# Sliding-window attention and a gated feed-forward block on one core: attention matmuls recut into 64x64 tiles, chunks 2 to 7 transposed on TensorE, output blocks moved later

## The chip, the cores and the metric

The kernel runs on one core of a Trainium2 chip. The core has TensorE (PE, matmuls; its weight loads are listed as PEld), VectorE (DVE), ScalarE (ACT), GpSimd (POOL) and SyncE (SP), and 16 DMA engines that all queues share. PE writes to eight PSUM banks of 128 partitions x 512 f32, which DVE and ACT read; everything else works on SBUF, 128 partitions wide. The metric is the device time of one execution in microseconds (us).

## The reference

```python
# q, k, v: (8, 8, 576, 64): batch, heads, positions, head size
scores = q @ k^T / 8, masked to 0 <= i - j < 64
attn   = softmax(scores)
x      = (attn @ v) laid out as 4608 tokens x 512
g      = x @ w_gate                      # 512 x 1536
out    = (g * sigmoid(g) * (x @ w_val)) @ w_out     # 1536 x 512, float32
```

All inputs and the output are float32 in memory; the kernel computes with bfloat16 operands and float32 sums.

## The kernel before

**Chunks and blocks.** The 4608 tokens are 36 chunks of 128 (n = 0 to 35) for the attention and 9 blocks of 512 (c = 0 to 8) for the feed-forward. A chunk holds all 8 heads.

**Attention of a chunk.** `S(n)` (L340) makes the scores transposed, keys on the partitions. For each half chunk of 64 queries (w) the window is the 128 keys from 64 before it; 16 matmuls hold 64 rows (head size) x 128 keys as weights and stream 64 queries. Even and odd heads (p) stand in the two halves of the rows and write two banks. ACT takes the exponential (L373), DVE multiplies by the 0/1 mask (L375); in the first four chunks a mask of -30000 is added by a matmul instead (L354). `AV(n)` (L377) has 16 matmuls of 128x128 weights (the probabilities) against 65 columns of v (64 and a column of ones): for each head one on `vb` (the values shifted by 64 tokens, L390) and one on `va` (L391). DVE takes the reciprocal of the sum (L397) and multiplies (L400) into `xb`. The probabilities are kept 192 wide with a zero middle so that both matmuls have all 128 columns. `X(n)` (L403) turns `xb` into a quarter of `xT`: by four PE transposes and a copy in the first six chunks, by a DMA transpose on SP's queue (L412) from chunk 6 on. `T(n)` (L324) turns k and q by DMA transposes on SP's queue (L332), from chunk 4 on; `shift_v` (L290) makes `vb` by two SP DMAs a chunk. The first two pairs of chunks are loaded as float32, cast, and transposed on PE (`first_loads`, `first_cast`, `first_T`).

**Feed-forward.** `F(c, f)` (L504) makes one of 12 row blocks of the hidden layer for 512 tokens: 4 + 4 matmuls of 512 columns (L479), tanh on ACT (L490), two DVE operations (L498, L501) into `hT`. `O(c, u)` (L528) makes 128 rows of the output: 12 matmuls (L538), a copy on ACT (L543), an ACT-queue DMA. `hT` is a ring of two (`NH`), so all of block c-1's outputs are made while block c is computed.

**Order.** The order on each engine is written out by hand in `opening` (L573) and `build` (L636); `_Graph` (L31) derives the semaphore waits from which buffer is read and written, and an instruction that waits holds everything behind it on its engine or queue. POOL's queue carries the float32-to-bfloat16 loads (k, q and v at L288, the two weights at L313, `Wo` at L318) in program order; a load waits for the last reader of its ring slot. SP's queue carries the transposes and the shifted values in order. In the main loop (blocks 2 to 8) each quarter u has F, AV(n), F, S(n+1), O(c-1, u), F on PE. PSUM banks: four for F, one for O (`"o"`), three for attention (`"a"`).

Of the kernel before, what the change touches and what calls it, by code (L numbers as in the profile page):

```python
# [9 lines left out]
T = B * S  # L10
# [20 lines left out]
class _Graph:  # L31
# [10 lines left out]
    def op(self, eng, fn, reads=(), writes=(), dma=False):  # L42
# [4 lines left out]
        for k in writes:  # L47
            for r in self.readers.get(k, ()):
                deps.setdefault(r.i, (r, "war"))
            for w in self.writers.get(k, ()):  # L50
                deps.setdefault(w.i, (w, "waw"))
        o = _Op(len(self.ops), eng, fn, list(deps.values()), dma)
# [8 lines left out]
    def emit(self):  # L61
# [7 lines left out]
        for o in self.ops:  # L69
# [16 lines left out]
            for d, kind in deps:  # L86
                if d.eng == e and not d.dma and (e == "pe" or kind != "raw") and not o.dma and e != "pool":
                    continue
                need(d)
# [60 lines left out]
class _Kernel:  # L150
# [5 lines left out]
    NH = 2  # L156
    NS = 4
    NO = 4

# [6 lines left out]
    def alloc(self):  # L166
# [9 lines left out]
        self.mask = sb("mask", 4 * 64)  # L176
        self.nmask = sb("nmask", 4 * 64)
# [3 lines left out]
        hd = lambda t: t[:, :].rearrange("p (h d) -> p h d", h=H)  # L181
        self.qn = ring("qn", self.NQ, DM)
        self.kn = ring("kn", self.NQ, DM)
        self.va = [hd(t) for t in ring("va", self.NV, H * 80)]
        self.vb = [hd(t) for t in ring("vb", self.NV, H * 80)]
        self.kT = sb("kT", 4 * (T + 64))[:, :].rearrange("p (c t) -> p c t", c=4)
        self.qT = sb("qT", 4 * self.NZ * 128)[:, :].rearrange("p (c t) -> p c t", c=4)
        self.wz = sb("wz", 512)
        self.pt = [t[:, :].rearrange("p (h x) -> p h x", h=H) for t in ring("pt", self.NP, H * 192)]
# [10 lines left out]
        self.fk = [f4(hT[1][:, 0:2048]), f4(hT[1][:, 2048:4096])]  # L200
        self.fq = [f4(hT[1][:, 4096:6144]), f4(xT[2][:, :])]
        h1 = lambda a: [("hT", 1, f) for f in range(4 * a, 4 * a + 4)]
        self.fkk = [h1(0), h1(1)]
        self.fqk = [h1(2), [("xT", 2, u) for u in range(4)]]
        c4 = lambda t: t[:, :].bitcast(BF).rearrange("p (j h d) -> p j h d", j=4, h=4)
        self.ck, self.cq = [c4(self.ost[0]), c4(self.ost[2])], [c4(self.ost[1]), c4(self.ost[3])]
        self.ckk, self.cqk = [[("ost", 0)], [("ost", 2)]], [[("ost", 1)], [("ost", 3)]]
        self.wup = sb("wup", 1, F32)
        self.ps = [nc.alloc_psum_tensor("ps%d" % i, [128, 512], F32) for i in range(8)]
        self.rot = {"f": ([0, 1, 2, 3], 0), "o": ([4], 0), "a": ([5, 6, 7], 0)}  # L210
# [28 lines left out]
    def init(self):  # L239
        g = self.g  # L240
        self.zero(self.wup[:, :], ["wup"])
        g.op("act", lambda e: e.activation(self.wup[:, :], self.wup[:, :], ACTF.Exp), writes=["wup"])
        self.zero(self.ident[:, :], ["ident"])
        self.zero(self.wz[:, :], ["wz"])
        self.zero(self.nmask[:, :], ["nmask"])
        self.init_va(0, 4)
        self.zero(self.kT[:, :, 0:64], [("kT", -1, 0), ("kT", -1, 1)])
        self.zero(self.vb[0][0:64, :, 0:66], [("vb", 0, 0)])
        for i in range(self.NP):
            self.zero(self.pt[i][:, :, 64:128], [("pt", i, 0), ("pt", i, 1)])  # L250
        self.zero(self.mask[:, :], ["mask"], 1.0)
# [5 lines left out]
    def init_ident(self, m, key):  # L257
        self.g.op("pool", lambda e: e.affine_select(
            out=m[:, :], in_=m[:, :], compare_op=ALU.not_equal, fill=1.0, base=0,
            pattern=[[-1, 128]], channel_multiplier=1), writes=[key])  # L260

    def init_mask(self, m, key, fill):
        mm = m[:, :].rearrange("p (a q) -> p a q", a=4)
        self.g.op("pool", lambda e: e.affine_select(
            out=mm, in_=mm, compare_op=ALU.is_gt, fill=fill, base=0,
            pattern=[[0, 4], [-1, 64]], channel_multiplier=1), writes=[key])
        self.g.op("pool", lambda e: e.affine_select(
            out=mm, in_=mm, compare_op=ALU.is_ge, fill=fill, base=64,
            pattern=[[0, 4], [1, 64]], channel_multiplier=-1), writes=[key])
        self.g.op("pool", lambda e: e.memset(m[0:64, 128:192], fill), writes=[key])  # L270
# [19 lines left out]
    def shift_v(self, n, eng="sp"):  # L290
        if n >= NCH:
            return
# [484 lines left out]
```

## Time and profile before

| What | us |
|---|---|
| Three runs | 366.23, 367.96, 367.74; median 367.74 |
| Span of the profiled execution (its own time) | 366.3 |
| PE busy | 335.8 (92%), 2617 matmuls |
| DVE / ACT / POOL busy | 223.2 (61%) / 131.5 (36%) / 108.7 (30%) |
| Matmuls of F (L479) | 116.3 + 115.6 |
| Matmuls of O (L538) | 96.1 |
| Matmuls of S (L360), of AV (L390, L391) | 15.3; 23.1 + 23.2 |
| Mean granted TensorE clock | 0.971 |

The profiled execution took as long as the fastest of the three runs; its span runs from the first to the last instruction. Busy time of PE counts overlapping matmuls once, and a matmul's record includes its way through the array, so a record of 0.19 us does not keep the next matmul waiting for 0.19 us: the distance between starts does. "issue" in a chain is time in which the engine waited for nothing that the profile shows. Times in the timeline are from the start of the span.

### The profile page before, as it was taken

Reading aid. Unit: us, or ns where it says so; the run is one execution under the profiler, and the core shown is the slowest. Engines: PE = TensorE matmul, PEld = TensorE weight load, DVE = VectorE, ACT = ScalarE, POOL = GpSimd, SP = SyncE. Lnnn points to the kernel's source line nnn. Section 1 sums busy time; section 2 is a strip of 40 time slices with the busy share of each in tenths; the row PEclk is TensorE's granted clock in tenths of the full one; section 3 lists DMA queues with packets and bytes.
Section 4 is the critical chain, followed back from the end, with each engine's and each line's share of the span. In section 5 each row is a group of like instructions: output and inputs, shape, how many; then the busy total and the mean of one; then the engine's idle time right before and its main releaser. Section 6 shows DMA issues by size and latency. Waiting matters only on the chain.

```text
span 366.3 us, 6689 instructions
## 1 busy us (share of the span) xinstructions
PE 335.8 (92%) x2617; PEld 170.8 (47%) x2617; DVE 223.2 (61%) x482; ACT 131.5 (36%) x234; POOL 108.7 (30%) x139
## 2 busy tenths in 40 slices
PE   7677976399859999899999999999999999999996
PEld 3354445365424444444444444444444444444444
DVE  5667887346446666666666666666666666545530
ACT  2343433124332343344433433334344433233221
POOL 8999614252055432222222433220000000000000
PEclk9789998889988999999999999999999999999999
DMA  9999999999999999999999999996433332101003
GB/s 161 227 182 153 180 183 147 156 173 188 163 169 164 162 152 137 155 134 130 149 143 147 149 132 145 140 144 103 91 90 91 95 77 44 44 35 54 29 29 117
DMA packets 176864, 47.30 MB, mean 129 GB/s; under 512 B 159360, under 2 KB 172352, under 8 KB 176832
## 3 DMA queue, kind: packets, MB, share of 16 engines
q0 software_dynamic: 113152, 17.83, 69.8%
q1 hardware_dynamic: 57952, 19.20, 31.6%
q10 hardware_dynamic: 5728, 9.83, 7.8%
q8 instruction: 21, 0.34, 0.4%
q14 instruction: 11, 0.09, 0.1%
HBM read 37.75 MB, written 9.44 MB: 129 GB/s over the span
## 4 chain that ended last, share of the span: by engine, by line
PE 83%; DVE 6%; DMA 6%; issue 3%; ACT 2%; SPq 1%; ACTq 0%; DVEq 0%
PE ps L479 48%; PE ps L538 25%; DMA qT<-qn 4%; PE ps L360 3%; PE ps L391 2%; PE ps L390 2%; DMA hT<-in_q_dram 2%; DVE xb L400 2%; DVE uu L498 1%; ACT sig L490 1%; PE ps L560 1%; DVE vb L234 1%; DVE kT L234 1%; PE ps L354 1%; DVE hT L501 1%
## 5 line engine op out<-in xcount | busy, mean ns | idle before, releaser
L498 DVE SCALAR_TENSOR_TENSOR uu<-sig,ps 128x512 bf16<-128x512 bf16 (+1 forms) x116 | 75.1, 647 | 96.7 <-ACT sig L490 96.2
L479 PE MATMUL ps<-xT,Wg 128*128 128x512 bf16 (+1 forms) x472 | 116.3, 370 | 9.6 <-issue 5.5
L479 PE MATMUL ps<-xT,Wv 128*128 128x512 bf16 (+1 forms) x472 | 115.6, 369 | 0.0
L490 ACT ACTIVATE sig<-ps 128x512 bf16<-128x512 f32 (+1 forms) x116 | 65.9, 568 | 115.2 <-PE ps L479 115.2
L538 PE MATMUL ps<-Wo,hT 128*128 128x512 bf16 x420 | 96.1, 380 | 0.0
L501 DVE SCALAR_TENSOR_TENSOR hT<-uu,ps 128x512 bf16<-128x512 bf16 (+1 forms) x116 | 75.4, 650 | 4.5 <-PE ps L479 0.5
L479 PEld LDWEIGHTS ps<-xT,Wv 128*128 128x128 bf16 x472 | 47.3, 100 | 49.2 <-issue 1.9
L479 PEld LDWEIGHTS ps<-xT,Wg 128*128 128x128 bf16 x472 | 44.0, 100 | 52.8 <-issue 7.7
L538 PEld LDWEIGHTS ps<-Wo,hT 128*128 128x128 bf16 x420 | 39.2, 98 | 44.9
L288 POOL DMA_DIRECT2D qn<-in_q_dram x36 | 30.3, 843 | 84.6 <-DMA qT<-qn 82.9
L373 ACT ACTIVATE pt<-ps 128x512 bf16<-128x512 f32 x72 | 39.0, 595 | 33.4 <-PE ps L360 32.9
L543 ACT ACTIVATE ost<-ps 128x512 f32<-128x512 f32 x35 | 20.9, 597 | 67.0 <-PE ps L538 67.0
L288 POOL DMA_DIRECT2D kn<-in_k_dram x36 | 30.4, 846 | 43.7 <-DMA kT<-kn 40.8
L288 POOL DMA_DIRECT2D va<-in_v_dram x40 | 34.3, 861 | 7.4 <-DMA Wo<-in_moe_w_out_dram 4.7
L400 DVE TENSOR_TENSOR xb<-ps,rc 128x256 bf16<-128x256 f32 x72 | 30.6, 425 | 2.5
L375 DVE TENSOR_TENSOR pt<-pt,mask 128x512 bf16<-128x512 bf16 x64 | 24.8, 420 | 11.2 <-ACT pt L373 10.7
L360 PE MATMUL ps<-qT,kT 64*128 64x64 bf16 x576 | 15.3, 195 | 9.2 <-issue 3.9
L390 PE MATMUL ps<-vb,pt 128*128 128x65 bf16 x288 | 23.1, 195 | 0.3 <-ACT pt L373 0.3
L391 PE MATMUL ps<-va,pt 128*128 128x65 bf16 x288 | 23.2, 195 | 0.0
L390 PEld LDWEIGHTS ps<-vb,pt 128*128 128x128 bf16 x288 | 20.7, 99 | 4.1 <-ACT pt L373 0.5
L360 PEld LDWEIGHTS ps<-qT,kT 64*128 64x128 bf16 x576 | 11.0, 97 | 23.7 <-DVE rc L397 9.8
L391 PEld LDWEIGHTS ps<-va,pt 128*128 128x128 bf16 x288 | 19.5, 99 | 3.4
(48 smaller groups left out, 76.9 us busy)
## 6 DMA issues: line engine op xcount, KB each, us to landing
out_dram<-ost ACTq DMA_DIRECT2D x35, 256.0 KB, 2.8
vb<-va SPq DMA_DIRECT2D x63, 80.0 KB, 3.3
va<-in_v_dram POOLq DMA_DIRECT2D x32, 128.0 KB, 6.4
kn<-in_k_dram POOLq DMA_DIRECT2D x28, 128.0 KB, 5.7
qn<-in_q_dram POOLq DMA_DIRECT2D x28, 128.0 KB, 4.9
Wo<-in_moe_w_out_dram POOLq DMA_DIRECT2D x2, 768.0 KB, 26.3
Wg<-in_moe_w_gate_dram POOLq DMA_DIRECT2D x5, 256.0 KB, 9.7
Wv<-in_moe_w_val_dram POOLq DMA_DIRECT2D x5, 256.0 KB, 11.3
```

The lines of the kernel that those rows point to most:

```text
L288: self.g.op("pool", lambda e, d=d, a=a: e.dma_start(d, a), writes=ks, dma=True)
L360: r = e.matmul(sv[p][:, w, c], self.kT[ps, c, k0:k0 + 128], self.qT[ps, c, self.qs(n, 64 * w, 64 * w + 64)], start=not bias, stop=not bias ...
L373: g.op("act", lambda e, po=po, p=p: e.activation(po, sv[p], ACTF.Exp, scale=SCALE), reads=[bx[p][1]], writes=[pk])
L375: g.op("dve", lambda e, po=po: e.tensor_tensor(po, po, m, ALU.mult), reads=[pk, "mask"], writes=[pk])
L390: e.matmul(av[:, j, :], pt[:, h, 0:128], vb[:, h, 0:65], start=True, stop=False)
L391: r = e.matmul(av[:, j, :], pt[:, h, 64:192], va[:, h, 0:65], start=False, stop=True)
L400: g.op("dve", lambda e, xo=xo, av=av, rb=rb: e.tensor_tensor(xo, av[:, :, 0:64], rb, ALU.mult), reads=[bk, ("rc", ir)], writes=[("xb", ix, ...
L479: r = e.matmul(bank[:, lo:hi], W[:, kk, f * 128:f * 128 + 128], xT[:, kk, lo:hi], start=(kk == 0), stop=(kk == NK - 1))
L490: self.g.op("act", lambda e: e.activation(sig[:, lo:hi], G[:, lo:hi], ACTF.Tanh, scale=0.5), reads=[gk], writes=[("sig", i)])
L498: g.op("dve", lambda e: e.scalar_tensor_tensor(uu[:, lo:hi], sig[:, lo:hi], 1.0, G[:, lo:hi], ALU.add, ALU.mult), reads=[("sig", i), gk], ...
L501: g.op("dve", lambda e: e.scalar_tensor_tensor(hT[:, f, lo:hi], uu[:, lo:hi], 0.5, V[:, lo:hi], ALU.mult, ALU.mult), reads=[("uu", i), vk] ...
L538: r = e.matmul(OB[:, :], hT[:, f, 128 * u:128 * u + 128], self.Wo[:, f, :], start=(f == 0), stop=(f == NF - 1))
```

## The change

- **64x64 tiles.** S has, for each pair of heads, one matmul of the chunk's first 64 keys against all 128 queries into the lower half of the partitions, and two of 64 keys (the last 64 of the chunk before, the last 64 of this one) against 64 queries each into the upper half: 24 matmuls of 64x64 weights. Keys no longer need a window that starts 64 early, so `kT` becomes a ring of eight chunks. AV has 32 matmuls of 64x64 weights in two phases of 16. Within a phase each half of the rows writes one bank; in the second phase the banks are exchanged, and its first matmul waits on PE's own semaphore until the first phase is done. `vb` and `shift_v` go: the values of the chunk before are read from `va`.
- **B(n)** puts S(n+1) between the two phases of AV(n), from chunk 8 on.
- **Chunks 2 to 7.** k and q are loaded two tokens to a partition (`load2`) and transposed on PE (`T2`: 16 transposes and two copies for each of k and q of two chunks). The float32 path is kept for chunks 0 and 1 alone. X of chunks 4 to 7 is by PE, its copy on ACT.
- **F** can take a half of the tokens for two row blocks at once, which share one bank, one tanh and one DVE pair; chunks 0 to 3 and block 1 are ordered by such halves.
- **Three hT.** O(0,0) closes block 1; after that the outputs run up to seven quarters behind, and six outputs and the divided last one stand at the end. The bank of O joins those of attention.
- **Loads** are put in another order: all gate and value weights before k and q of chunks 4 and 5; `Wo` behind the loads of chunks 8 to 11.

```diff
@@ op, emit @@
-    def op(self, eng, fn, reads=(), writes=(), dma=False):
+    def op(self, eng, fn, reads=(), writes=(), dma=False, after=None):
...
+        if after is not None:
+            deps[after.i] = (after, "sync")
...
-                if d.eng == e and not d.dma and (e == "pe" or kind != "raw") and not o.dma and e != "pool":
+                if d.eng == e and not d.dma and kind != "sync" and (e == "pe" or kind != "raw") and not o.dma and e != "pool":
...
-    NH = 2
+    NH = 3
...
-        self.vb = [hd(t) for t in ring("vb", self.NV, H * 80)]
-        self.kT = sb("kT", 4 * (T + 64))[:, :].rearrange("p (c t) -> p c t", c=4)
+        self.qs2 = [pair(t) for t in ring("qs", 2, 2 * DM)]
+        self.ks2 = [pair(t) for t in ring("ks", 2, 2 * DM)]
+        self.kT = sb("kT", 4 * self.NZ * 128)[:, :].rearrange("p (c t) -> p c t", c=4)
-        self.rot = {"f": ([0, 1, 2, 3], 0), "o": ([4], 0), "a": ([5, 6, 7], 0)}
+        self.rot = {"f": ([0, 1, 2, 3], 0), "a": ([4, 5, 6, 7], 0)}
...
-    def shift_v(self, n, eng="sp"):
...
+    def load2(self, st, x):
+        src, dst = (self.k, self.ks2[st % 2]) if x == "k" else (self.q, self.qs2[st % 2])
+        parts = list(self.segs(256 * st, 256))
+        for j, (r, b, s, L) in enumerate(parts):
+            d = dst[r // 2:(r + L) // 2].rearrange("p h j d -> p h (j d)")
+            a = src[b, :, s:s + L, :].rearrange("h (p j) d -> p h (j d)", j=2)
+            ks = [("s2", x, st % 2, j)] if len(parts) > 1 else [("s2", x, st % 2, 0), ("s2", x, st % 2, 1)]
+            self.g.op("pool", lambda e, d=d, a=a: e.dma_start(d, a), writes=ks, dma=True)
...
+    def T2(self, st, x, engs):
+        g = self.g
+        src = (self.ks2 if x == "k" else self.qs2)[st % 2]
+        dst = self.kT if x == "k" else self.qT
+        z0 = (2 * st) % self.NZ
+        for cc in range(2):
+            bank, bk = self.bank("a")
+            tb = bank[:, 0:256].bitcast(BF).rearrange("p (c j t) -> p c j t", c=2, j=2)
+
+            def pe(e, cc=cc, tb=tb):
+                for c in range(2):
+                    for j in range(2):
+                        for p in range(2):
+                            r = e.transpose(tb[64 * p:64 * p + 64, c, j, :], src[:, 4 * cc + 2 * c + p, j, :], self.ident[:, :])
+                return r
+
+            g.op("pe", pe, reads=["ident", ("s2", x, st % 2, 0), ("s2", x, st % 2, 1)], writes=[bk])
+            d = dst[:, 2 * cc:2 * cc + 2, 128 * z0:128 * z0 + 256].rearrange("p c (t j) -> p c t j", j=2)
+            a = tb.rearrange("p c j t -> p c t j")
+            self.copy(engs[cc], d, a, [bk], [(x + "T", z, cc) for z in (z0, z0 + 1)])
...
-            for w in range(2):
-                k0 = 128 * n + 64 * w
-                for c in range(4):
+                    e.matmul(sv[p], self.ident[:, :], nm, start=True, stop=False, skip_group_check=True)
+            kw = dict(start=not bias, stop=True, skip_group_check=True)
+            for c in range(4):
+                for p in range(2):
+                    ps = slice(64 * p, 64 * p + 64)
+                    e.matmul(sv[p][0:64, c, :], self.kT[ps, c, self.zs(n, 0, 64)], self.qT[ps, c, self.zs(n)], **kw)
+                for ks, a in ((lk, 0), (self.zs(n, 64, 128), 64)):
                     for p in range(2):
                         ps = slice(64 * p, 64 * p + 64)
-                        r = e.matmul(sv[p][:, w, c], self.kT[ps, c, k0:k0 + 128],
-                                     self.qT[ps, c, self.qs(n, 64 * w, 64 * w + 64)],
-                                     start=not bias, stop=not bias or (w == 1 and c == 3))
+                        r = e.matmul(sv[p][64:128, c, a:a + 64], self.kT[ps, c, ks], self.qT[ps, c, self.zs(n, a, a + 64)], **kw)
             return r
...
-    def AV(self, n):
...
-                    e.matmul(av[:, j, :], pt[:, h, 0:128], vb[:, h, 0:65], start=True, stop=False)
-                    r = e.matmul(av[:, j, :], pt[:, h, 64:192], va[:, h, 0:65], start=False, stop=True)
...
+    def AVmm(self, st, phase):
+        n, bx, av, done = st
+        iv, jv, ip = n % self.NV, (n - 1) % self.NV, n % self.NP
+        va, vb, pt = self.va[iv], self.va[jv], self.pt[ip]
+
+        def pe(e):
+            for j in range(4):
+                for r in range(2):
+                    p = r if phase == 0 else 1 - r
+                    h = 2 * j + p
+                    for c in range(2):
+                        if n == 0 and r == 1 and c == 0:
+                            continue
+                        first = j == 0 and (phase == 0 or (n == 0 and c == 0 and r == 0))
+                        rows = slice(64 * r, 64 * r + 64)
+                        vv = vb if (r == 1 and c == 0) else va
+                        x = e.matmul(av[p][64 * c:64 * c + 64, j, :], pt[rows, h, 64 * c:64 * c + 64], vv[rows, h, 0:65],
+                                     start=first, stop=phase == 1, skip_group_check=True)
+            return x
+
+        rd = [("pt", ip, 0), ("pt", ip, 1)]
+        for i in {iv, jv} if n else {iv}:
+            rd += [("va", i), ("va", i, 0), ("va", i, 1)]
+        done.append(self.g.op("pe", pe, reads=rd, writes=[b[1] for b in bx], after=done[0] if phase else None))
...
+    def B(self, n):
+        st = self.AVa(n)
+        self.AVmm(st, 0)
+        if n + 1 < NCH:
+            self.S(n + 1)
+        self.AVmm(st, 1)
+        self.AVn(st)
...
-    def Fmm(self, bank, bk, W, wk, c, f, lo, hi):
...
-    def Fa(self, c, f):
...
-    def Fb(self, c, f, b):
...
+    def F(self, c, fs, half=None):
+        g = self.g
+        lo, hi = (0, 512) if half is None else (256 * half, 256 * half + 256)
...
-        OB, ok = self.bank("o")
+        OB, ok = self.bank("a")
...
+    def loads(self):
         W = lambda a, b: (self.load_w("g", a, b), self.load_w("v", a, b))
+        kq = lambda st: (self.load2(st, "k"), self.load2(st, "q"))
+        self.first_loads()
         self.init()
         self.load(0, "v")
         self.load(1, "v")
+        self.init_ident()
         W(0, 2)
+        self.init_mask()
+        kq(1)
+        W(2, 4)
         self.load(2, "v")
         self.load(3, "v")
         W(4, 6)
         W(6, 8)
+        W(8, 10)
+        W(10, 12)
+        kq(2)
+        self.load(4, "v")
         self.load(5, "v")
...
+    def more_loads(self):
+        self.load2(3, "k")
+        self.load2(3, "q")
+        self.load(6, "v")
+        self.load(7, "v")
+        for n in range(8, 12):
+            self.load(n)
         self.load_wo(0, 6)
         self.load_wo(6, 12)
-        self.load(8)
-        self.load(9)
-
+        self.load(12)
...
+        F(0, (0, 1), 0)
+        T2(1, "k", ("act", "dve"))
+        T2(1, "q", ("act", "dve"))
+        F(0, (2, 3), 0)
+        S(2, True)
+        S(3, True)
+        AV(2)
+        X(2, "act")
+        AV(3)
+        X(3, "act")
         self.init_va(4, self.NV)
+        self.more_loads()
+        F(0, (4, 5), 0)
+        F(0, (0, 1), 1)
+        F(0, (6, 7), 0)
+        F(0, (2, 3), 1)
+        F(0, (4, 5), 1)
+        F(0, (6, 7), 1)
+        T2(2, "k", ("act", "act"))
+        T2(2, "q", ("act", "act"))
+        F(0, (8,))
+        S(4)
+        S(5)
+        F(0, (9,))
+        AV(4)
+        AV(5)
         self.load(13)
+        F(0, (10,))
+        X(4, "act")
+        X(5, "act")
+        F(0, (11,))
+        F(1, (0, 1), 0)
+        T2(3, "k", ("act", "act"))
+        T2(3, "q", ("act", "act"))
+        F(1, (2, 3), 0)
+        S(6)
+        S(7)
+        for n in (8, 9):
+            self.T(n, "k")
+            self.T(n, "q")
+        F(1, (4, 5), 0)
+        AV(6)
+        AV(7)
+        F(1, (6, 7), 0)
+        X(6, "act")
+        X(7, "act")
+        F(1, (8, 9), 0)
+        self.T(10, "k")
+        self.T(10, "q")
+        F(1, (10, 11), 0)
+        F(1, (0, 1), 1)
+        S(8)
+        F(1, (2, 3), 1)
+        self.B(8)
+        self.X(8)
+        self.T(11, "k")
+        self.T(11, "q")
+        F(1, (4, 5), 1)
+        self.B(9)
+        self.X(9)
+        self.T(12, "k")
+        self.T(12, "q")
+        self.load(14)
+        F(1, (6, 7), 1)
+        self.B(10)
+        self.X(10)
+        self.T(13, "k")
+        self.T(13, "q")
+        self.load(15)
+        F(1, (8, 9), 1)
+        self.B(11)
+        self.X(11)
+        self.T(14, "k")
+        self.T(14, "q")
+        self.load(16)
+        F(1, (10, 11), 1)
+        self.load(17)
+        self.O(0, 0)
         for c in range(2, NFC):
             for u in range(4):
                 n = 4 * c + u + 4
+                if n < NCH:
+                    self.B(n)
+                    self.T(n + 3, "k")
+                    self.T(n + 3, "q")
+                    self.X(n)
+                    self.load(n + 6)
+                F(c, (3 * u,))
+                F(c, (3 * u + 1,))
+                i = 4 * (c - 2) + u + 1
+                self.O(i // 4, i % 4)
+                F(c, (3 * u + 2,))
+        self.banks("a", [4, 5, 6, 7, 0, 1, 2, 3])
+        for i in range(4 * (NFC - 2) + 1, T // 128 - 1):
+            self.O(i // 4, i % 4)
         self.O_last(NFC - 1, 3)```
```

## The prediction

> **What bounds the kernel now.** I read the chain that ended last, then the busy time by stretches, then the matmuls in order of time.
>
> Two lines of the page, busy time by engine and the chain by engine:
>
> ```profile
> PE 335.8 (92%) x2617; PEld 170.8 (47%) x2617; DVE 223.2 (61%) x482; ACT 131.5 (36%) x234; POOL 108.7 (30%) x139
> ...
> PE 83%; DVE 6%; DMA 6%; issue 3%; ACT 2%; SPq 1%; ACTq 0%; DVEq 0%
> ```
>
> PE is the chain, so its own work counts in full; 17% is waiting. Where the waiting lies (length, then PE busy with matmuls in brackets, PEld, DVE, ACT, POOL, granted clock, DMA share, GB/s):
>
> ```profile
> 19.00:31.00 12.00, 8.67 (x119) 6.33 (x118) 6.57 (x15) 4.64 (x9) 11.83 (x16) 0.92 1.86 177
> 31.00:47.00 16.00, 15.87 (x111) 7.34 (x109) 14.39 (x28) 6.76 (x13) 12.08 (x14) 1.00 1.80 169
> 47.00:61.00 14.00, 9.52 (x112) 6.54 (x112) 11.61 (x31) 4.45 (x10) 2.33 (x3) 1.00 1.39 164
> 61.00:73.00 12.00, 6.24 (x65) 4.91 (x66) 5.19 (x14) 2.51 (x6) 4.37 (x7) 0.82 2.23 156
> ...
> 90.00:108.00 18.00, 12.30 (x139) 6.84 (x138) 9.27 (x23) 4.66 (x10) 4.04 (x5) 0.95 1.50 174
> 108.00:319.00 211.00, 209.96 (x1611) 100.86 (x1610) 137.69 (x288) 82.66 (x143) 48.77 (x59) 0.99 1.01 123
> ```
>
> From 19 to 108 us PE is idle for about 20 us, after 108 hardly at all. The chain names the waits (start, length, what):
>
> ```profile
> 46.82 14.32 DMA qT<-qn
> ...
> 68.27 4.63 issue
> ...
> 105.16 2.09 issue
> ...
> 116.27 0.34 PE ps L360 x16
> 116.61 2.70 PE ps L538 x12
> 119.31 3.45 PE ps L479 x16
> 123.25 1.73 PE ps L479 x8
> 124.97 0.34 PE ps L360 x16
> ```
>
> The transposed q of chunk 7 lands 14.3 us after its issue; the two others are PE in front of transposes on SP's queue. The last five lines are a steady quarter: 124.97 - 116.27 = 8.70 us, of which three F (5.18) and one O (2.59) are 7.77; S and AV of a chunk together cost **0.93**. Call that cost a. How S and O follow one another:
>
> ```profile
> 186.72 0.38 PE L479 MATMUL ps<-xT,Wv 128*128 128x512 bf16 x1
> 187.03 0.41 PE L360 MATMUL ps<-qT,kT 64*128 64x64 bf16 x16
> 187.38 2.76 PE L538 MATMUL ps<-Wo,hT 128*128 128x512 bf16 x12
> ```
>
> Sixteen score matmuls of 0.19 us fit in 0.41, so their starts lie 0.22 apart from first to last: 0.22/15 = 14.5 ns each, 29 ns for a pair. 64 columns alone need that much, so two row halves work side by side, weight loads included. F's last start is 186.72, plus 0.216 for 512 columns gives 186.94: 0.1 us lost into the 64-row cut; from the last score start (187.24) to O 0.135 out of it.
>
> **The change, part by part.** The sum is made against the span 366.3. It has the form: start t0 of F(2,0) + everything behind it.
>
> *Behind t0.* 24 quarters of 7.77 = 186.5, block 8 without attention 4 x 7.77 = 31.1, six O at the end 15.5 (three more than now), the divided last O with copy and DMA 5.45 (360.83 to 366.3), 1 for a stall at a block's border such as now (one quarter at 142 takes 9.9, +1.2), and 23 times a: 239.6 + 23a. The same addition for before, with t0 = 111.2 plus 0.85 for F(2,0) at half clock, three O, 24 AV and 23 S gives 366.3.
>
> *The new a.* S has per group of two heads two matmuls of 128 columns and four of 64, AV eight sets of four matmuls of 65. **Lower end:** all four tiles side by side at the 29 ns of the score pairs: S 4 x 58 = 0.23, AV 8 x 29 = 0.24, cuts in and out 0.235, 0.05 for the second phase's wait (the first phase's last record is 0.19 long and S covers 0.23): 0.755. **Upper end:** no overlap at all: S 8 x 56 + 16 x 29 ns = 0.91, AV 32 x 29 = 0.94, cuts: 2.09. Between them lies overlap of the row halves alone, as now: S 0.46, AV 0.47: 1.17. Column halves side by side appear in no row of before. I take **0.80**, near the lower end, since the nearest row (the score pairs) shows weights and streams of two tiles fully parallel.
>
> A rule against the change: the Trainium skill, "TensorEngine Tiling (Array Packing)", Restrictions, says that column tiling switches fast weight load off, and "TensorE: Matmul & The Clock Gate", LDWEIGHTS, gives columns / 1.2 ns for a plain load. By it 64 columns take 53 ns and every set of four is bound by them: an estimate of 0.235 + 16 x 0.053 = 1.09, about the time of before. In today's rows the loads of 128 columns follow each other at 29 ns per row half and bind nothing; no row has a 64-column load.
>
> *The opening, up to t0* (start of each step on PE; F halves cost 1.74, sixteen steps of 0.109):
> - Before the first F (18.8): the shifts of v by DVE go (0.52 each), AV waits for both exponentials: 18.6.
> - F 20.5 (cold clock), T2 of chunks 2, 3: 32 transposes, bounded by 29 ns (score pace) and 57 ns (four X transposes in 0.40): 0.9 to 1.8, taken 1.6 with cuts: 22.1. F 23.9. S(2), S(3) 25.7. AV and X of 2 and 3: each X waits for four DVE operations (1.2 us) as now (26.8 and 28.7): 30.5.
> - Six F halves: 41.0. T2 of 4, 5: 42.6. F, S(4), S(5), F: 46.9. AV(4), AV(5): 0.9 of waiting for masks, 48.7. F, then X(4), X(5), 1.4 of waiting for DVE: 52.3. F, F, T2, F, S(6), S(7), F: 61.7. AV, F, X of 6 and 7, again 2.3 of waiting: 67.1. Three F halves, S(8), F, B(8): 75.3. F, B(9): 77.8. F: 79.6.
> - **The new wait:** SP's queue has X(8), T(11)k, T(11)q in order. xb(8) is ready 2.7 after B(8), behind two masks (0.42) and two reciprocals and products (1.2): 78.0. With 1.2 to 1.3 per issue and 4.1 to landing, T(11)q lands at 84.6; S(11) inside B(10) waits 4.8 for it, and behind it the whole of PE. B(10) ends at 85.2, an F at half clock 88.0, B(11) 89.0, F and O(0,0) 93.4; T(13) and X(11) hold B(12) and F(2,0) another 1.2: 95.6.
> - 1.5 for cold clock not counted: **t0 = 97**.
>
> Do loads come in time? By the queue table the POOL packets take 0.698 x 366.3 x 16 / 113152 = 36 ns of one engine. Before, about 31,000 of them ran until `Wo` had landed (POOL's issue at 60.42 waited for it): 570 a us from 5 us on. After, those of k, q 4 and 5 end the first 14,300 (30 us, needed at 41), k, q 6, 7 and v up to 7 the first 20,500 (41, needed at 56), k, q 10 28,700 (55, needed at 77), `Wo` 65 (needed at 91). These are hidden; with no cover the whole chain shifts by what they are late. POOL's order moves past nothing that it waits on: chunks 8 to 13 have free slots.
>
> *What goes:* 8 DMA transposes of T, 63 shifts on SP, two X on SP; none is on the steady chain (108 to 319). Their gain is the 14.3 and the waits behind it, inside t0. ACT gains ten copies of 0.6 in the opening, with 36% share covered; DVE has 3 x 1.38 + 0.84 + 1.2 = 6.2 of 8.6 us a quarter. hT[c%3] was read out a quarter before block c needs it: no wait.
>
> **Sum:** 366.3 - (112.0 - 97) + 7.8 (three O moved behind t0) - 0.9 (S and AV of one more chunk ahead of it) - 23 x 0.13 = 3.0 gives 355.2. The median stands 1.4 above the profiled span: **356.5**.
>
> **Rivals.**
> 1. *Slower: the column halves do not overlap (or their weights do not).* a applies 34.5 times (11.5 in the opening). Pairs only, a = 1.17: + 12.8, 368 in the span, 369.2; no overlap, 2.09: about 400. It decides from a = 0.80 + 11.1/34.5 = 1.12. For it: no column cut in any row; against: rows overlap perfectly. The same engine then shows 24 or 32 matmuls spread over 0.5 us or more.
> 2. *The opening stays bound by DMA.* A transpose issued while `Wo` moves took 14.3 us; six (T(8) to T(10)) now stand near it. From the point where q of chunk 10 lands after 77, each us shows: up to 10, 366.5.
> 3. *Phase two drains the array.* If S does not hide the wait, 0.25 (0.19 record and a semaphore) 34 times: 361 in the span.
> 4. *All goes well:* a at 0.755 and T(11) hidden: 349.
>
> **How the numbers follow.** The forecast's own case 0.47, rival 1 0.28, rival 2 0.15, rival 3 0.06, rival 4 0.04. Half a per cent (1.8 us) is about what a measurement of this kernel can tell. Faster: 0.46 + 0.05 + 0.05 + 0.04 = 0.60; within half a per cent 0.01 + 0.04 (rival 1 with pairs alone) + 0.06 + 0.01 = 0.12; slower 0.24 + 0.04 = 0.28. The range runs from rival 4 less 2 us, 347, to a = 1.37 (356.5 + 34.5 x 0.57), 376; a in the region of 2 (0.1) stays out. The likeliest case alone spans 350 to 363.
>
> **What would show it.** A steady quarter of 8.57 (7.77 + 0.80), score and AV starts four within a few ns; F(2,0) at 95 to 99; a wait of S(11) for DMA kT or qT near 80; no wait of PE for a DMA before that; 15.5 us of O ahead of the last. Wrong if the quarter exceeds 8.9, if matmuls of different column halves start 29 ns or more apart, or if T2 or S(8) waits for loads.

## The result, and the profile after

| | median us | lowest to highest | ratio to before (95%) |
|---|---|---|---|
| before | 367.74 | 366.23 to 368.67, 5 runs | |
| changed | 363.02 | 362.9 to 365.37, 5 runs | 0.9888 [0.9854, 0.9922] |

The change makes the kernel faster by 1.1%. The forecast was 3.1% (356.5 us): the direction is right, and about a third of the gain came. The profiled execution of the changed kernel took 365.37 us with a span of 363.0; the other four had spans of 360.6 to 360.8. In all five the time lies 2.2 to 2.4 above the span, so the span that answers to the median is about 360.7. The ratios leave out executions more than 1.5% above the fastest of the same kernel, here one alone, of 368.29 us, when the changed kernel was measured once more.

Busy time by engine, and the chain by engine and by line, of the changed kernel:

```profile
PE 332.9 (92%) x3608; PEld 177.7 (49%) x3641; DVE 212.1 (58%) x446; ACT 137.4 (38%) x239; POOL 105.0 (29%) x135
...
PE 69%; ACT 10%; DVE 9%; DMA 6%; issue 3%; ACTq 2%; SPq 1%
PE ps L536 39%; PE ps L562 24%; DVE uu L544 5%; ACT sig L542 4%; ACT ost L567 4%; DVE xb L437 2%; ACTq L569 2%; DMA hT<-in_q_dram 2%; DMA qT<-qn 2%; DMA xT<-xb 2%; ACT pt L392 2%; PE ps L417 1%; PE ps L345 1%; PE ps L470 1%; PE ps L584 1%
```

About a thousand more matmuls keep PE busy for 2.9 us less. Behind the first load (`hT<-in_q_dram`, 2% as before), the DMA waits of the chain are now the transposes of q and `xb`, 2% of the span each. That ACT and DVE hold 10% and 9% of the chain is taken up at the end.

Where the waiting lies, in the stretches of the prediction (length, then PE busy with matmuls in brackets, PEld, DVE, ACT, POOL, granted clock, DMA share, GB/s):

```profile
19.00:31.00 12.00, 10.49 (x152) 7.29 (x152) 4.50 (x8) 4.97 (x9) 9.88 (x14) 0.69 1.52 193
31.00:47.00 16.00, 13.45 (x128) 10.88 (x129) 9.29 (x24) 4.26 (x8) 15.56 (x19) 0.79 2.19 161
47.00:61.00 14.00, 12.65 (x205) 7.73 (x206) 10.84 (x23) 8.41 (x16) 5.75 (x7) 1.00 1.70 157
61.00:73.00 12.00, 11.15 (x221) 9.01 (x220) 8.90 (x21) 7.78 (x15) 3.51 (x4) 1.00 2.21 163
...
90.00:108.00 18.00, 11.01 (x151) 6.37 (x152) 7.03 (x18) 4.02 (x8) 6.23 (x8) 0.78 1.64 147
```

PE is now busy for 12.65 and 11.15 us where it was for 9.52 and 6.24 (47 to 61 and 61 to 73): the long wait for q is gone. From 90 to 108 it is idle for 7 us, more than before, and the clock there fell to 0.78. Two stretches early on run at 0.69 and 0.79, where before had 0.92 and 1.00.

What PE waited for (total, times, longest):

```profile
PE ps L470 <- DVE xb L437: 6.6, 6, 1.3
PE ps L378 <- DMA qT<-qn: 5.2, 2, 3.8
PE ps L536 <- DVE uu L544: 3.9, 23, 0.3
PE ps L536 <- DMA xT<-xb: 2.7, 1, 2.7
```

The first is X on PE (L470): 1.3 each in chunks 0 to 3 and 0.7 in chunks 5 and 7, which the prediction had counted. The second and fourth are the new waits, three in all. The third comes once in a quarter, 0.17 us each, and is taken up at the end too.

Those waits in the chain (start, length, what):

```profile
86.07 1.19 SPq L463
87.30 1.26 SPq L329
88.61 6.63 DMA qT<-qn
95.28 0.26 PE ps L378
...
95.99 1.09 ACT pt L392 x2
...
98.66 6.48 DMA xT<-xb
105.14 0.45 issue
105.58 4.82 PE ps L536 x15
```

T(12)q is issued on SP's queue (`SPq`) behind X(9) and T(12)k, and lands 6.6 us later; S(12) (95.28) waits for it. Then the scores, exponential (L392), mask and products, and the transpose X(11), again 6.5 us, hold block 2's first F. Of that F's first four records one is missing, so block 2 starts at 105.1: this is t0.

The same place on PE, in order of time (start, length, what, in brackets the idle time ahead and what ended it):

```profile
85.52 0.32 PE L417 MATMUL ps<-va,pt 64*64 64x65 bf16 x16 [0.76 <-DVE xb L437]
87.22 0.24 PE L378 MATMUL ps<-qT,kT 64*64 64x128 bf16 x2 [1.39 <-DMA qT<-qn]
...
87.73 1.69 PE L536 MATMUL ps<-xT,Wg 128*128 128x256 bf16 x8
89.22 1.91 PE L536 MATMUL ps<-xT,Wv 128*128 128x256 bf16 x8
...
95.28 0.32 PE L378 MATMUL ps<-qT,kT 64*64 64x128 bf16 x2 [3.79 <-DMA qT<-qn]
...
96.08 1.89 PE L536 MATMUL ps<-xT,Wg 128*128 128x256 bf16 x8
...
199.93 0.32 PE L417 MATMUL ps<-va,pt 64*64 64x65 bf16 x16
```

Read three things. The first phase of AV stands in front of each wait, so S(11) and S(12) hold the whole of PE from inside B. The F half behind the wait of 1.39 takes from 87.73 to 91.06, 3.3 us where 1.74 is usual: the clock is at half for most of it. And sixteen AV matmuls of 0.19 fit in 0.32: (0.32 - 0.19) / 15 = 9 ns from start to start, about 35 ns for a set of four. All four tiles work at once.

The steady quarter (start, length, what):

```profile
118.93 2.60 PE ps L562 x12
...
127.45 2.60 PE ps L562 x12
...
135.97 2.60 PE ps L562 x12
```

127.45 - 118.93 = 8.52 us, as is 135.97 - 127.45. It was 8.70 before and forecast as 8.57.

### The profile page after: what moved, and what is told of

It is laid out like the page before. It is cut to its first block, busy times and chain, and to the rows that moved or that the text cites. A ratio compares the mean times of both kernels' runs of the same rounds, so it can differ in the third digit from the quotient of the medians.

```text
span 363.0 us, 8541 instructions
## 1 busy us (share of the span) xinstructions
PE 332.9 (92%) x3608; PEld 177.7 (49%) x3641; DVE 212.1 (58%) x446; ACT 137.4 (38%) x239; POOL 105.0 (29%) x135
## 4 chain that ended last, share of the span: by engine, by line
PE 69%; ACT 10%; DVE 9%; DMA 6%; issue 3%; ACTq 2%; SPq 1%
PE ps L536 39%; PE ps L562 24%; DVE uu L544 5%; ACT sig L542 4%; ACT ost L567 4%; DVE xb L437 2%; ACTq L569 2%; DMA hT<-in_q_dram 2%; DMA qT<-qn 2%; DMA xT<-xb 2%; ACT pt L392 2%; PE ps L417 1%; PE ps L345 1%; PE ps L470 1%; PE ps L584 1%
## 5 line engine op out<-in xcount | busy, mean ns | idle before, releaser
L544 DVE SCALAR_TENSOR_TENSOR uu<-sig,ps 128x512 bf16<-128x512 bf16 x108 | 73.8, 684 | 98.5 <-ACT sig L542 98.3
L536 PE MATMUL ps<-xT,Wg 128*128 128x512 bf16 (+1 forms) x484 | 110.1, 358 | 7.8 <-DVE uu L544 3.9
L542 ACT ACTIVATE sig<-ps 128x512 bf16<-128x512 f32 x108 | 64.6, 598 | 74.3 <-PE ps L536 73.7
L546 DVE SCALAR_TENSOR_TENSOR hT<-uu,ps 128x512 bf16<-128x512 bf16 x108 | 74.2, 687 | 5.2 <-PE ps L536 1.6
L567 ACT ACTIVATE ost<-ps 128x512 f32<-128x512 f32 x35 | 20.9, 597 | 95.7 <-PE ps L562 95.7
L296 POOL DMA_DIRECT2D kn<-in_k_dram x31 | 26.9, 875 | 98.7 <-DMA kT<-kn 98.7
L392 ACT ACTIVATE pt<-ps 128x512 bf16<-128x512 f32 x72 | 38.8, 596 | 30.9 <-PE ps L382 30.9
L437 DVE TENSOR_TENSOR xb<-ps,rc 128x256 bf16<-128x256 f32 x72 | 30.6, 424 | 2.5
L417 PE MATMUL ps<-va,pt 64*64 64x65 bf16 x1144 | 23.5, 200 | 2.4 <-DVE xb L437 1.5
L417 PEld LDWEIGHTS ps<-va,pt 64*64 64x64 bf16 x1144 | 15.8, 109 | 15.9 <-issue 10.4
L378 PE MATMUL ps<-qT,kT 64*64 64x128 bf16 x288 | 14.7, 225 | 5.6 <-DMA qT<-qn 5.2
L434 DVE RECIPROCAL rc<-ps 128x4 f32<-128x4 f32 x72 | 12.5, 174 | 8.3 <-PE ps L417 8.3
L382 PE MATMUL ps<-qT,kT 64*64 64x64 bf16 x576 | 15.6, 197 | 0.0
L378 PEld LDWEIGHTS ps<-qT,kT 64*64 64x64 bf16 x288 | 9.6, 110 | 9.3 <-DMA qT<-qn 5.4
```

The lines of the kernel that those rows point to most:

```text
L296: self.g.op("pool", lambda e, d=d, a=a: e.dma_start(d, a), writes=ks, dma=True)
L378: e.matmul(sv[p][0:64, c, :], self.kT[ps, c, self.zs(n, 0, 64)], self.qT[ps, c, self.zs(n)], **kw)
L392: g.op("act", lambda e, po=po, p=p: e.activation(po, sv[p], ACTF.Exp, scale=SCALE), reads=[bx[p][1]], writes=[pk])
L417: x = e.matmul(av[p][64 * c:64 * c + 64, j, :], pt[rows, h, 64 * c:64 * c + 64], vv[rows, h, 0:65], start=first, stop=phase == 1, skip_gro ...
L437: g.op("dve", lambda e, xo=xo, p=p, rb=rb: e.tensor_tensor(xo, av[p][:, :, 0:64], rb, ALU.mult), reads=[bk, ("rc", ir)], writes=[("xb", ix ...
L536: r = e.matmul(bank[:, a * n:a * n + n], W[:, kk, f * 128:f * 128 + 128], xT[:, kk, lo:hi], start=(kk == 0), stop=(kk == NK - 1))
```

## The experiments

Three theories were set against each other for what the opening cost beyond the forecast. *Queue*: T(11), T(12) and T(13) stand behind X(8), X(9) and X(10) on SP's queue, which works in order, so S(11) and S(12) inside B wait for transposes whose data lay ready. *Clock*: the early stretches at 0.5 to 0.8 of the clock shift everything behind them. *Contention*: the transposes land late, because each landing of T releases a load into the same DMA engines. Other runs price the parts of the change. The ratios to before are compared.

### The transposes ahead of X(8)

```diff
-        self.T(10, "k")
-        self.T(10, "q")
+        for n in (10, 11, 12, 13):
+            self.T(n, "k")
+            self.T(n, "q")
...
-        self.T(11, "k")
-        self.T(11, "q")
```

(The two later pairs, of 12 and 13, go likewise.)

> Edit: the DMA transposes of k and q of chunks 11, 12 and 13 stand on SP's queue directly behind those of chunk 10, ahead of X(8); nothing else moves. Queue theory (the late t0 is the wait of S(11), S(12), S(13) and F(2,0) behind X on SP's queue, and the half clock after each of these waits): no wait of PE for qT, F(2,0) at 96 to 99 instead of 105.6, 354 to 357 us. Clock theory (the late t0 comes from half clock before 40 us): F(2,0) at 102 to 104, 360 to 362 us.

Measured: 357.22 us, 0.9739 [0.9687, 0.979]. By the ratios that is 1.5%, or 5.5 us, below the changed kernel (the intervals do not touch). PE's waits from 70 to 110 us:

```profile
PE ps L417 <- DVE xb L437: 2.0, 3, 0.8
PE ps L536 <- DMA xT<-xb: 1.7, 1, 1.7
```

No wait for qT is left. Block 2 starts 20.9 us after S(8) (74.7 to 95.6), against 28.5 in the changed kernel (76.6 to 105.1). The queue theory holds. What stood in the way is seen on SP's queue of the changed kernel (start, length of the issue, what). Between 49 and 82 us it has nothing, then one issue directly behind another:

```profile
47.89 1.22 SPq L329 DMA_TRANSPOSE qT<-qn  x1
...
82.13 1.20 SPq L463 DMA_TRANSPOSE xT<-xb  x1
83.37 1.26 SPq L329 DMA_TRANSPOSE kT<-kn  x1
84.68 1.26 SPq L329 DMA_TRANSPOSE qT<-qn  x1
```

The queue stood still for 33 us behind X(8), which waits for `xb` of chunk 8. On the same queue with the transposes ahead of it, T(11)k and T(13)q are issued at 51.5 and 72.0:

```profile
51.52 1.76 SPq L329 DMA_TRANSPOSE kT<-kn  x1
...
72.01 1.24 SPq L329 DMA_TRANSPOSE qT<-qn  x1
```

So, in this execution, k and q of chunks 11 to 13 had been loaded by 72, ten us before the changed kernel's queue moved on.

### The outputs moved into the gaps

The waits are kept, and work that was due later is put in front of them: O(0,0) before B(10), O(0,1) before B(11), O(0,2) at the end of block 1. The later outputs move up by two.

```diff
+        self.O(0, 0)
...
+        self.O(0, 1)
...
-        self.O(0, 0)
+        self.O(0, 2)
...
-                i = 4 * (c - 2) + u + 1
+                i = 4 * (c - 2) + u + 3
```

> Edit: O(0,0), O(0,1), O(0,2) stand in front of B(10), B(11) and at the end of block 1, so that PE works in the waits for qT; the outputs run five quarters behind instead of seven and two fewer stand at the end. Queue theory: the waits are real idle time, so about 5 us of output work costs nothing: 356 to 359 us, and the half clock of 88 to 98 us goes. Clock theory: the waits are small beside the clock's share, 361 to 363 us.

Measured: 358.22 us, 0.976 [0.9715, 0.9806]. From S(8) to S(14) passed 36.1 us (75.35 to 111.45) with two O (5.2 us) more in between than in the changed kernel, which took 38.2. One wait of 2.5 us, of S(12), is left. Waits at the same place, filled with other work, give nearly what their removal gives.

### Matmuls on zeros early

Twelve matmuls on a zero tile into an unused bank, two to three at a time, stand around AV and X of chunks 0 and 1 and before the first F, where PE waits, to hold the clock up.

```diff
+    def fill(self, count):
+        bank, bk = self.ps[3], ("ps", 3)
+        def pe(e):
+            for _ in range(count):
+                r = e.matmul(bank[:, :], self.wz[:, 0:128], self.wz[:, :], start=True, stop=True)
+            return r
+        self.g.op("pe", pe, reads=["wz"], writes=[bk])
```

> Edit: twelve dummy matmuls of 512 columns on zeros (a bank that nothing uses then) stand in the waits of AV and X of chunks 0 and 1, before the first F. Clock theory (the first F, T2, F at half clock from 20.6 to 28 us because PE had too many pauses before): the first F takes 1.75 instead of 3.60, T2 about 1.0 instead of 1.85, all later steps 2 to 4 us earlier, 359 to 361 us. Queue theory: the opening's later waits swallow it, since T(11) stands behind X(8), whose own time moves with PE: also earlier, but by no more than 2, 361 to 363 us. If the clock does not follow such pauses: 363 to 365 us.

Measured: 362.8 us, 0.9892 [0.9842, 0.9942]: no gain. In its profiled execution the clock did rise (the number behind POOL's, 0.83 and 1.00; the first execution of the changed kernel has 0.52 and 0.69):

```profile
9.00:19.00 10.00, 7.53 (x130) 3.44 (x130) 2.76 (x9) 4.00 (x7) 10.00 (x14) 0.83 1.72 185
19.00:31.00 12.00, 9.31 (x192) 6.26 (x190) 6.00 (x14) 5.54 (x10) 11.30 (x15) 1.00 1.51 193
```

There S(8) came at 73.4 instead of 76.6. The median did not move with it. The clock theory explains one profiled execution, not the median.

### The changed kernel once more

> Edit: none; the changed kernel once more, to see how much of the late F(2,0) belongs to one execution. If the 17 us at half clock from 9.5 to 26.5 us are a matter of the moment at which the clock's windows start, another execution has another pattern and S(8) moves by 1 to 3 us; the waits for qT and xT between S(10) and S(14) stay, S(14) 35 to 38 us behind S(8); 361 to 365 us. If both belong to the program, S(8) is at 76.6 again.

Measured: 361.85 us (359.44 to 364.63, three executions), 0.9857 [0.9798, 0.9915]; the profiled execution took 359.44. In the same two stretches it was granted 0.76 and 0.78:

```profile
9.00:19.00 10.00, 5.77 (x124) 3.51 (x125) 2.72 (x9) 3.43 (x7) 10.00 (x15) 0.76 1.72 183
19.00:31.00 12.00, 8.99 (x181) 6.18 (x180) 6.50 (x17) 4.94 (x9) 12.00 (x16) 0.78 1.53 193
```

S(8) came at 72.0, where the forecast had 72.3. So the same program runs its opening 4.6 us faster or slower, and the clock it is granted accounts for that. Counted as either full or half, the means from 9 to 47 us make about 24 us at half clock in the first execution (2 x (10 x 0.48 + 12 x 0.31 + 16 x 0.21)) and about 14 in this one (0.88 from 31 to 47). Ten us at half clock lose five. The waits for DMA are of the same kind in both, here two for q (4.6 in all, the longest 3.2) and 1.8 for xT.

### The small tiles alone

The kernel before, with S and AV cut into 64x64 tiles and nothing else: S and AV stand where they stood, the shifts are gone, the loads and transposes are as before.

```diff
-                    e.matmul(av[:, j, :], pt[:, h, 0:128], vb[:, h, 0:65], start=True, stop=False)
-                    r = e.matmul(av[:, j, :], pt[:, h, 64:192], va[:, h, 0:65], start=False, stop=True)
...
+                        x = e.matmul(av[p][64 * c:64 * c + 64, j, :], pt[rows, h, 64 * c:64 * c + 64], vv[rows, h, 0:65],
+                                     start=first, stop=phase == 1, skip_group_check=True)
```

> Edit: the kernel before with the 64x64 tiles of S and AV alone (no shifted values, mask by 128 columns, second phase of AV behind PE's own semaphore), its order, its loads and its DMA transposes kept; S and AV stay apart. Theory that the tiles are worth their time by themselves: the steady quarter falls from 8.70 to 8.5, about 361 us. Theory that they pay only with S between the phases (two more cuts in and out, 0.235, and 0.25 for the drained array): quarter 8.75 to 8.9, 366 to 370 us.

Measured: 377.16 us, 1.0274 [1.0229, 1.0319], slower than either theory had it. Its chain in the steady part:

```profile
161.72 0.28 PE ps L389 x16
...
162.05 0.32 PE ps L389 x16
162.37 1.83 PE ps L496 x8
...
164.58 2.69 PE ps L555 x12
...
173.58 2.70 PE ps L555 x12
```

The quarter is 173.58 - 164.58 = 9.00, against 8.70 before: the tiles by themselves cost 0.30 a quarter, although four work at once (sixteen AV in 0.28 to 0.32). Twenty-four quarters make 7.2 of the 10 us.

### S behind AV

The changed kernel, with S(n+1) behind both phases of AV(n) instead of between them.

```diff
-        st = self.AVa(n)
-        self.AVmm(st, 0)
+        self.AV(n)
...
-        self.AVmm(st, 1)
-        self.AVn(st)
```

> Edit: B(n) is AV(n) with both phases and then S(n+1), still in one 64x64 stretch. Theory that S hides the drain between the phases (first run of the tiles alone: S and AV of a chunk 1.23 apart, 0.755 together): the quarter grows from 8.52 by the drain alone, about 0.25, to 8.77; 28 times, 369 to 371 us. Theory that the second pair of cuts in and out was the price there: quarter 8.55 at most, 363 to 364 us.

Measured: 365.38 us, 0.9941 [0.9908, 0.9973]. The total is a miss, the quarter is not:

```profile
157.31 2.59 PE ps L559 x12
...
166.13 2.59 PE ps L559 x12
```

166.13 - 157.31 = 8.82, which is 0.30 over 8.52. Over 22 quarters that is 6.6 us, but the median lost only 0.9941 - 0.9888 = 0.5%, 1.9 us. The remaining 4.7 must have come back ahead of the first of these quarters. The chain of the profiled execution has F(2,0) and F(2,1) here:

```profile
100.81 3.56 PE ps L533 x16
```

S(8) stands at 75.4 there, so block 2 starts 25.4 us behind it instead of 28.5, and its first two F take 3.5 us at full clock, where the changed kernel took 5.1 (105.1 to 110.2). That is 3.1 + 1.6 = 4.7; against the other execution of the changed kernel it is 1.5 + 1.8. AV(n) and its products no longer stand behind S(n+1)'s wait for q, and no wait for xT is left before block 2. That this is what gave the gain is argued from the traces, not shown by a run of its own.

### Chunks 4 to 7 by DMA transposes again

```diff
-        self.load2(3, "k")
-        self.load2(3, "q")
-        self.load(6, "v")
-        self.load(7, "v")
+        self.load(6)
+        self.load(7)
...
+        for n in (4, 5):
+            self.T(n, "k")
+            self.T(n, "q")
...
-        T2(2, "k", ("act", "act"))
-        T2(2, "q", ("act", "act"))
```

> Edit: k and q of chunks 4 to 7 are loaded by single tokens and turned by DMA transposes again, X by PE and everything else kept (T2 for chunks 2 and 3 stays). Theory that the PE transposes took the 14.3 us wait away: S(4) or S(6) waits 5 to 12 us for qT, 368 to 375 us. Rival, that the other order of loads (Wo behind chunks 8 to 11) took it away: no wait there, 2 us of T2 saved, 360 to 363 us.

Measured: 373.53 us, 1.0165 [1.0111, 1.0219]. The chain goes through a transpose of q that takes 11.28 us, and PE waits for q in four places (total, times, longest):

```profile
PE ps L378 <- DMA qT<-qn: 17.8, 4, 9.0
```

In the changed kernel's order, T2 of chunks 4 to 7 is worth 1.0165 - 0.9888 = 2.8%, 10 us: more than twice what the change as a whole brought.

### Larger rings

If a landing of T releases a load that slows the next transpose, more slots (9 for q and k, 14 for v, instead of 6 and 10) put these loads earlier. What the theory rests on is POOL's queue in the changed kernel (issue of a load of k; 14.86 us idle ahead, ended by the landing of T(11)k):

```profile
86.22 0.88 POOL L296 DMA_DIRECT2D kn<-in_k_dram  x1 [14.86 <-DMA kT<-kn]
```

```diff
-    NQ = 6
-    NV = 10
+    NQ = 9
+    NV = 14
```

> Edit: rings of nine instead of six for k and q and of fourteen instead of ten for v, so that loads 17 to 19 are not released by the landing of T(11) to T(13); the order of every queue is kept. Contention theory (T(12) and X(11) land in 6.6 and 6.5 us because the load that the transpose before them released shares the DMA engines): landings of 3 to 4.5 us, S(12) at 92 to 93 instead of 95.3, S(14) at 109 to 112 instead of 114.8, 358 to 361 us. Rival, that the transposes wait for each other on the queue: no landing changes, 363 us.

Measured: 359.88 us (357.51 to 362.51), 0.9787 [0.9714, 0.9859]. The total is where the contention theory had it, but its interval just touches the changed kernel's [0.9854, 0.9922], so the gain is at the edge of the noise. The single transposes do not bear the theory out one by one. T(11)q and T(13)q are now on the chain:

```profile
84.24 4.76 DMA qT<-qn
...
95.09 6.05 DMA qT<-qn
```

T(11)q took 4.8 us (2.5 in the changed kernel) and S(11) waits 3.8 for it; T(13)q took 6.1 (3.2), and S(13) waits 1.8. T(12)q fell from 6.6 to 4.0, and the waits of S(12) and for X(11) are gone.

That the loads play a part is likely, not shown; how they slow one transpose and not another stays open.

### Put together

The early transposes, the zero matmuls and O(0,1) beside O(0,0) in one kernel; the same without the zero matmuls; the first with larger rings.

> Edit: the changed kernel with the transposes of chunks 11 to 13 ahead of X(8), the dummy matmuls in the first waits, and O(0,1) beside O(0,0) at the end of block 1, in front of F(2,0). Queue and clock theory together: the 9.5 us of the first at S(14), 2 to 3 of the second, 1.7 of the wait for xT: 349 to 352 us in the span, 352 to 355 in the median. If the two gains are one (both only move X(8)): 354 to 357 us.

> Edit: transposes of chunks 11 to 13 ahead of X(8) and O(0,1) beside O(0,0) in front of F(2,0); no dummy matmuls. Queue theory: like the first run with the wait for xT (1.7) filled by work: 352 in the span, 355 to 357 in the median. Against the run with all three this shows what the dummy matmuls bring: by the clock theory 2 to 3 us, so this one is slower by that; if they bring nothing at the end, the same.

> Edit: the run with all three and rings of nine and fourteen. Contention theory: loads 17 to 19 no longer fall on X(8) to X(11); 1 to 2 us less than the run with all three, 353 to 355 us. If the loads simply move earlier, onto the transposes of chunks 8 to 13: no gain, 355 to 358 us.

| | median us | ratio to before (95%) |
|---|---|---|
| transposes early | 357.22 | 0.9739 [0.9687, 0.979] |
| all three | 356.36 | 0.9691 [0.9642, 0.9741] |
| without zero matmuls | 355.93 | 0.9698 [0.9668, 0.9729] |
| all three, larger rings | 359.35 | 0.9783 [0.9744, 0.9822] |

The versions with and without the zero matmuls cannot be told apart; the one without them is 3.0% below before and 1.9% below the changed kernel. The zero matmuls bring nothing here either: with a gain of their own all three were to take 352 to 355 us, without one 354 to 357. Whether the second O at the end of block 1 brings anything over the early transposes lies inside the intervals. Larger rings, which may have helped the changed kernel as it was, cost 0.9% once the queue's order is mended, more than either expectation had (358 us at most); why stays open.

## Why the prediction was right in direction and wrong in size

**Behind t0: right.** Forecast 239.6 + 23 x 0.80 = 258.0; measured 363.0 - 105.1 = 257.9, and 353.4 - 95.6 = 257.8 with the transposes early. That it fits to 0.1 is luck. The first two F of block 2 ran at half clock in part and took 5.1 us instead of 3.5, which the sum had not. Against that, the cost a came out at 8.52 - 7.77 = 0.75, the lower end, and the 1 us for a stall at a block's border did not come. Rival 1 falls: the starts of four tiles lie about 9 ns apart, and a set of four takes about 35 ns, where the pair of before took 29. The rule weighed against the change does not show in these rows: the Trainium skill, "TensorE: Matmul & The Clock Gate", LDWEIGHTS, by which a plain load of 64 columns is estimated at 53 ns and would bind each set of four.

**Rival 3's price was right, its place was not the changed kernel.** The wait between the phases costs 0.30 a quarter (forecast 0.25) where nothing covers it, as S behind AV shows; in B the scores cover it. The tiles alone cost another 0.18 over that (9.00 against 8.82), with S and AV each in a cut of its own: that these are the 0.235 of cuts that the prediction counted is argued from the nearness of the numbers. So the small tiles and B are one change: the first alone loses 10 us.

**Rival 2, the opening bound by DMA: fell up to 82 us.** T2 and S(8) wait for no load. T2 of chunks 4 to 7 is worth 10 us, as chunks 4 to 7 by DMA transposes show; the prediction had put its gain at the transpose of 14.3 us and the waits behind it. The 32 transposes of two chunks took 1.01 at full clock (1.6 forecast).

**t0: wrong, and this is the step that failed.** Forecast 97, measured 105.1 in the first profiled execution and 98.9 in the other one. With 257.9 behind it, the span of 360.7 that answers to the median puts t0 near 102.8, an estimate. The 8.1 of the first fall into two halves.

Up to S(8): 76.6 for 72.3. The other execution of the same kernel has 72.0. In the first, about 24 us of the opening ran at half clock, in the other about 14; the prediction had carried over the clock of the one execution of before, about 7 (2 x (10 x 0.24 + 12 x 0.08), with 0.76 from 9 to 19 us). PE's order up to S(8) is the same in seven profiled executions (the two of the changed kernel, and those with outputs in the gaps, S behind AV, larger rings, early transposes, and early transposes with O(0,1) but no zero matmuls). In them S(8) stands at 72.0 to 77.0, in the middle at 75.4. So the term was about 3 us too small, and varies by 5 from one execution to the next. Whether the change lowers the clock here or the one profile of before had a good moment stays open.

From S(8) to t0: 28.5 for 24.7 (26.9 in the other execution). By its terms:
- *"The new wait"* was found where it was put, but its share was mis-sized. S(11) waits 1.4, not 4.8, since T(11)q landed after 2.5 and not 4.1 and PE came to it 1.5 later, by the next item. S(12) waits 3.8, and X(11) holds F(2,0) for 2.3 (2.7 in the table less the missing record), where the prediction had *"another 1.2"* for T(13) and X(11). The sum is 7.5 for 6.0. It had seen one transpose behind one X, and not that T(12) stands behind X(9) in the same way.
- Products: AV(9) and AV(10) wait 0.74 and 0.76 for the products of the chunk before (`xb`, L437). AV writes the PSUM banks that these products still read (four banks, two for S and two for AV of each B), and on DVE they stand behind the mask of the scores made inside the same B. This was priced at nothing: 1.5. The lines of the chain ahead of B(10) are below.
- Half clock: the two F halves behind the waits took 3.3 and 3.0 instead of 1.74, 2.8 in all. The prediction had 1.1 in its half F and *"1.5 for cold clock not counted"*: 0.2 more.
- The bank of O: inside B(12), S(13) waits 0.44 for the copy of O(0,0) (`ost`, L567), since O now takes its bank from the same four. This was priced at nothing: 0.4.

That makes 1.5 + 1.5 + 0.2 + 0.4 = 3.6 of 3.8. The rest is not accounted for. The chain of the changed kernel between the scores in B(9) and AV(10) (start, length, what):

```profile
82.82 1.09 ACT pt L392 x2
83.94 0.42 DVE pt L394
...
85.08 0.30 issue
```

From the exponential's start to the end of the products at 85.08 pass 2.3 us. PE has one F half (1.74) to put beside it in block 1, where a steady quarter has an O and three F.

**What the median missed.** 363.02 is 6.5 over 356.5, and the early transposes alone take 5.5 away. But the forecast already held 6.0 of these waits, so this is not the whole answer: with T(11) hidden, rival 4 had foreseen 349, and the measured time of that case is 357.22. In its profiled execution S(8) came 2.4 later than forecast, 2.0 went to AV's waits for products and 1.7 to X(11): 6.1 of these 8.2, none of which the early transposes remove. The opening was thus taken too short in three places at once: the clock, the products behind the masks, and the chain of waits on the queue.

The step from span to median was too short as well. The profiled execution of before was taken as one of the fastest, with 1.4 from its span to the median. In later runs of that kernel an execution's time lies 1.8 to 2.1 above its own span, so the profiled one took about 368 us itself; in the changed kernel the distance is 2.3, so 0.9 of the 6.5 lies here.

## What to carry to other kernels

When a dependent step is pulled inside another (S inside AV), list every producer that the step has on an in-order queue, and every element that stands ahead of each: here a queue idle for 33 us held transposes whose inputs were loaded ten us before it moved on, and moving six lines was worth more than the whole change had brought. Small tiles that run four at a time gained here only with other matmuls between their dependent phases: the quarter was 8.52 with them, 8.82 without and 8.70 before. Take the clock of an opening from more than one execution before a shift of a few us there is put down to an edit.

## What the runs showed of the hardware

- **Four tiles at once.** 64x64 matmuls of 65 columns start about 9 ns apart; a set of four needs about 35 ns, loads of weights included, where a pair of 64x128 needed 29 before.
- **A dependent phase costs 0.30 us** when PE must wait for its own last matmul (quarters of 8.82 and 8.52).
- **The clock falls after a wait.** Behind waits of 1.4 and 3.8 us of PE an F half took 3.3 and 3.0 us instead of 1.74, and behind one of 2.3 two whole F took 5.1 instead of 3.5. With the early transposes and O(0,1) beside O(0,0), without zero matmuls, where these waits are gone or filled, the mean granted clock from 73 to 108 us is 1.00. Early on, one program was granted different clocks in two executions. Its mean from 9 to 19 us was 0.52 in one and 0.76 in the other, from 19 to 31 us 0.69 and 0.78.
- **DMA transposes of k and q, all of one size, land after 2.4 to 11.9 us** in the changed kernel, those of chunks 11 to 13 after 2.5 to 6.6. Loads released at the same time were near the long ones of these; the cause was not isolated.
- **A chain can leave the bounding engine for a gap that is hardly there.** In the steady part the chain of the changed kernel goes from O through ACT and `uu` to the next F, as in these lines:

```profile
199.32 0.61 ACT sig L542
...
199.95 0.70 DVE uu L544
...
200.80 3.40 PE ps L536 x15
```

F has sixteen matmuls and fifteen records there: the first is missing, so PE was not idle up to 200.80, and PE did AV and S from 199.93 on. A faster ACT or DVE would gain at most those gaps, which the waits put at 0.17 us each. With the transposes early, the steady part shows F with all sixteen records, no such wait, and the same 8.52: the gaps are those of the missing record.
